# One kernel, the same 1738 operations in another order: linear attention and a squared-ReLU FFN on one NeuronCore

## The chip, the cores and the metric

The kernel runs on one core of one Trainium2 chip. The metric is the device time of one execution in microseconds, as the median over runs. Everything that follows is read from one profiled execution of the kernel before the change.

## What is computed

```python
def phi(x):                                   # x: (8, 8, 576, 64), w_phi: (64, 128)
    proj = np.einsum('bhsd,df->bhsf', x, w_phi)
    proj = proj - np.max(np.abs(proj), axis=-1, keepdims=True)
    return np.concatenate([np.exp(proj), np.exp(-proj)], axis=-1)
q_p, k_p = phi(q), phi(k)
kv  = np.einsum('bhsf,bhsd->bhfd', k_p, v)
z   = np.sum(k_p, axis=2)
num = np.einsum('bhsf,bhfd->bhsd', q_p, kv)
den = np.einsum('bhsf,bhf->bhs', q_p, z)[..., None] + 1e-06
x   = (num / den).transpose(0, 2, 1, 3).reshape(4608, 512)
h   = np.maximum(x @ w_in, 0.0)               # w_in: (512, 2048)
out = (h * h) @ w_out                         # w_out: (2048, 512)
```

Eight batches of 576 tokens with eight heads go through the attention, and all 4608 tokens then go through the FFN. Inputs and output are float32 in HBM; the matmuls run in bfloat16.

## The kernel before, in words

**Staging.** Each batch has 512 tokens in the main part and 64 at its end. The FFN works on nine chunks of 512 tokens: chunk c (0 to 7) is the main part of batch c, and chunk 8 gathers the 64-token ends of all batches (tile `xS`). While the attention of batch c + 1 runs, the FFN of chunk c runs between its pieces. TensorE takes both in one instruction stream.

**Attention of one batch.** k, q and v are loaded by GpSimd's queue (`load`, `load_q`; lines 245, 253, 265, 274) into double-buffered tiles `xk`, `xq`, `xv`, with a cast to bfloat16. k and q have to stand head dimension first. For batches 0 and 1 TensorE does that (L316, operations Txk and Txq, with copies Cxk and Cxq from PSUM by VectorE or ScalarE, L190 and L192). From batch 2 on one DMA transpose each on SyncE's queue does it (L326, Xxk and Xxq). `project` (L342; L369 and L494 in the first batch) multiplies with `w_phi`. Its contraction is only 64 deep, so its matmuls use 64 of the 128 rows, and two of them with different rows follow one another in pairs. The program calls such operations `tiled`: Pk, Pq, and Fq (L572). VectorE takes the maximum of absolute values (L376, L397, L501, L534: Mk, Mq), and ScalarE the two exponentials (L385, L403, L547, L587). ScalarE's em makes the factors of v, VectorE scales v with them (L430: V, V4), and KV (L458, L463) sums k features times v. NA and NB (L651; L602 in the first chunk) multiply the features of q with it; between them VectorE scales by en (L663: SA). VectorE then divides (L673, L677: rd, xo). The result is transposed into `xT`, by TensorE for batch 0 (L630, L693) and by a DMA transpose on SyncE's queue for the others (L711: Xx). For batches 4 to 7 the features of q are made token first and are transposed by a DMA as well (L551: Xf).

**FFN of one chunk.** F1 (L797) makes four accumulating matmuls of 128 x 512 into one PSUM bank. Relu (L774 on ScalarE or L776 on VectorE) moves the bank to `hr`, and VectorE squares it (L783). F2 (L891) makes four of the sixteen accumulating matmuls of an output tile; after the last, a copy to `ot` (three buffers, L190 or L192) and a store (L909, L906) follow on SyncE's queue. Chunk 0 goes in smaller pieces, f1a, f1b, f1 and f1p (L822, L808, L836), so that it can begin before the attention of batch 0 is done. The very last output tile is split in columns (L855, L869, L871, L878).

**What sets the order.** Nothing is scheduled while the kernel is built. Each piece of work is added to a `Plan` as an operation with a number (its `seq`), an engine, and the values that it reads and writes. Five tables at the end of the file then say what becomes of it:

- `ORDER` lists all 1738 operations. Each engine takes its own in that order, held by dependencies that `pin` adds (L135). Within one engine nothing overtakes.
- `BASES` gives each PSUM tile its bank (eight banks, shared by all uses).
- `STATES` says for each copy or relu that may run on either ScalarE or VectorE which of the two takes it.
- `GATES` makes a load of batches 2 to 7 wait for one named operation before GpSimd issues it.
- `FILL` puts matmuls on a zero tile (L964) ahead of some TensorE operations.

```python
def arrange(self):
    for op in self.ops:
        if op.alt is not None and STATES[op.group] == "1":
            op.eng, op.occ, op.lat = op.alt
    for g, b in zip(self.banks, BASES):
        g.base = int(b)
    return [self.ops[i] for i in ORDER]
```

The numbers used in the prediction: 85, 74, 50, 41 and 63 are the five k transposes of batch 0 on TensorE; 9 and 13 the loads of k that 41 and 63 read; 15 and 20 the two halves of q of batch 0; 329 is the first f1a. 315, 1079 and 1276 are Xx transposes, each the last or next to last of its chunk. 1178 is a load of v for batch 6, and 1295 a relu. 555 and 716 are output stores, 733 an output copy, and 1709 to 1723 the last stores ahead of the split tile's.

Of the kernel before, what the change touches and what calls it, by code (L numbers as in the profile page):

```python
# [107 lines left out]
def kernel(  # L108
# [952 lines left out]
)  # L1061
STATES = (
    '0000000101000111101000110010000000000000010000011100110000100010001000101001010001000010110010100010'
    '0000100100100101010000000000100100100001100100101000011101000000000100101011101000000100010110001000'
    '1101100110001011100000011011000'
)
GATES = {
# [46 lines left out]
```

## Time and profile before

| | |
|---|---|
| median of 3 runs | 354.33 us (352.88 to 354.97) |
| profiled execution, its own time | 353.94 us |
| its span, first to last instruction | 352.2 us |
| TensorE, VectorE, ScalarE, GpSimd busy | 97%, 76%, 66%, 27% of the span |
| moved by DMA | 49.05 MB, 139 GB/s over the span |
| mean granted TensorE clock | 0.995 |

The page gives busy time by engine and slice, the chain of work that ended last, and groups of instructions by source line. Views of the trace give windows, waits and the timeline. In the timeline a row has the start and the duration in us, then engine, line, operation and tiles, with the number of instructions that were merged into it; a matmul's duration includes its tail, so a row reaches beyond the start of the next. "SPq" and the like are issuing instructions. A line like L797 is that of kernel.py.

### The profile page before, as it was taken

How to read it: one execution, taken by the hardware profiler on the slowest of the kernel's cores; microseconds unless marked ns; L12 is line 12 of the kernel's file. 1: busy time of each engine (PE TensorE's matmuls, PEld its weight loads, DVE VectorE, ACT ScalarE, POOL GpSimd, SP SyncE). 2: the span in 40 equal slices, each digit the busy share in tenths (PEclk: the TensorE clock that was granted, in tenths of full speed). 3: DMA queues.
4: the chain of work that ended last, by engine and by line, in shares of the span. 5: the costliest groups of instructions: out<-in, count | busy, mean ns of one | idle time of the engine just before them, and what ended most of it. 6: DMA issues, size and time to landing. Idle time of an engine off the chain costs nothing.

```text
span 352.2 us, 8392 instructions
## 1 busy us (share of the span) xinstructions
PE 341.5 (97%) x3343; PEld 192.0 (55%) x3343; DVE 268.9 (76%) x513; ACT 233.3 (66%) x439; POOL 96.2 (27%) x144
## 2 busy tenths in 40 slices
PE   6999999999999999999999999999999999999995
PEld 6778866544644555445545555455555554444443
DVE  4899997889887989689979887877989653564150
ACT  3999997789885776976597785895596503212111
POOL 8673461282461636021421302040100000000000
PEclk9999999999999999999999999999999999999999
DMA  8999999999999899997999999999857431100115
GB/s 92 172 196 202 201 155 168 159 122 167 162 130 189 138 150 151 165 201 152 163 140 202 165 212 140 214 106 179 155 117 157 96 87 67 60 2 0 71 50 120
DMA packets 133623, 49.05 MB, mean 139 GB/s; under 512 B 102096, under 2 KB 129104, under 8 KB 133584
## 3 DMA queue, kind: packets, MB, share of 16 engines
q0 software_dynamic: 45232, 18.36, 46.0%
q1 hardware_dynamic: 88112, 29.99, 44.3%
q8 instruction: 26, 0.43, 0.5%
q10 hardware_dynamic: 240, 0.16, 0.2%
q14 instruction: 13, 0.11, 0.1%
HBM read 36.77 MB, written 9.44 MB: 131 GB/s over the span
## 4 chain that ended last, share of the span: by engine, by line
PE 77%; DVE 10%; ACT 5%; DMA 5%; issue 2%; SPq 0%; DVEq 0%; ACTq 0%; POOLq 0%
PE psum L797 27%; PE psum L891 27%; PE psum L651 4%; PE psum L458 4%; PE psum L342 4%; PE psum L836 2%; DMA out_dram<-ot 2%; DVE va L430 2%; DMA xT<-xo 2%; DVE mk L397 1%; ACT hr L774 1%; DMA xk<-in_k_dram 1%; DVE hr L776 1%; PE psum L572 1%; DVE h L783 1%
## 5 line engine op out<-in xcount | busy, mean ns | idle before, releaser
L891 PE MATMUL psum<-wout,h 128*128 128x512 bf16 x560 | 134.9, 379 | 0.2 <-ACT ot L192 0.2
L797 PE MATMUL psum<-xT,win 128*128 128x512 bf16 x448 | 106.9, 379 | 1.4 <-DVE hr L776 0.8
L774 ACT ACTIVATE hr<-psum 128x512 bf16<-128x512 f32 x103 | 59.8, 596 | 54.5 <-PE psum L797 36.8
L891 PEld LDWEIGHTS <-h 128*128 128x128 bf16 x560 | 50.4, 97 | 54.6 <-issue 0.9
L797 PEld LDWEIGHTS <-win 128*128 128x128 bf16 x512 | 47.6, 97 | 54.3 <-issue 2.7
L783 DVE TENSOR_TENSOR h<-hr 128x512 bf16<-128x512 bf16 x144 | 56.6, 415 | 20.6 <-ACT hr L774 19.8
L547 ACT ACTIVATE qf<-psum 128x1024 bf16<-128x1024 f32 (+1 forms) x40 | 36.5, 938 | 12.3 <-DVE mq L534 11.3
L397 DVE TENSOR_REDUCE mk<-psum 128x8 f32<-128x1024 f32 (+1 forms) x35 | 38.6, 1110 | 4.6 <-PE psum L342 4.5
L587 ACT ACTIVATE qpn<-psum 128x1024 bf16<-128x1024 f32 (+1 forms) x40 | 36.7, 938 | 5.7 <-PE psum L572 4.9
L403 ACT ACTIVATE kp<-psum 128x1024 bf16<-128x1024 f32 (+1 forms) x35 | 32.7, 935 | 9.3 <-DVE mk L397 9.2
L651 PEld LDWEIGHTS <-qpn 128*128 128x128 bf16 x624 | 27.8, 98 | 13.9 <-issue 1.0
L663 DVE TENSOR_TENSOR psum<-psum,en 128x520 f32<-128x520 f32 (+1 forms) x39 | 27.2, 701 | 9.5 <-PE psum L651 5.6
L776 DVE TENSOR_SCALAR hr<-psum 128x512 bf16<-128x512 f32 x41 | 27.8, 685 | 6.7 <-PE psum L797 6.2
L403 ACT ACTIVATE kn<-psum 128x1024 bf16<-128x1024 f32 (+1 forms) x35 | 32.8, 937 | 0.0
L651 PE MATMUL psum<-kv,qpn 128*128 128x65 bf16 x624 | 31.1, 193 | 0.0
L430 DVE TENSOR_TENSOR va<-xv,va 64x256 bf16<-64x256 bf16 (+2 forms) x66 | 30.1, 471 | 0.9 <-ACT va L422 0.2
L245 POOL DMA_DIRECT2D xv<-in_v_dram x27 | 19.7, 734 | 36.0 <-DVE h L783 11.8
L245 POOL DMA_DIRECT2D xk<-in_k_dram x28 | 20.6, 740 | 31.6 <-ACT va L422 20.0
L677 DVE TENSOR_TENSOR xo<-psum,rden 128x512 bf16<-128x512 f32 (+1 forms) x39 | 26.7, 686 | 1.4 <-DMA xT<-xo 0.7
L265 POOL DMA_DIRECT2D xq<-in_q_dram x24 | 17.4, 725 | 33.0 <-ACT hr L774 13.7
L534 DVE TENSOR_REDUCE mq<-psum 128x8 f32<-128x1024 f32 (+1 forms) x20 | 22.3, 1113 | 2.9 <-PE psum L342 2.7
L501 DVE TENSOR_REDUCE mq<-psum 128x8 f32<-128x1024 f32 (+1 forms) x20 | 22.0, 1111 | 0.9 <-PE psum L342 0.8
(79 smaller groups left out, 383.5 us busy)
## 6 DMA issues: line engine op xcount, KB each, us to landing
out_dram<-ot SPq DMA_DIRECT2D x32, 256.0 KB, 3.1
xk<-in_k_dram POOLq DMA_DIRECT2D x26, 128.0 KB, 4.6
xq<-in_q_dram POOLq DMA_DIRECT2D x24, 128.0 KB, 4.8
xv<-in_v_dram POOLq DMA_DIRECT2D x24, 128.0 KB, 4.5
win<-in_moe_w_in_dram POOLq DMA_DIRECT2D x4, 512.0 KB, 9.2
wout<-in_moe_w_out_dram POOLq DMA_DIRECT2D x4, 512.0 KB, 14.0
xq<-in_q_dram POOLq DMA_DIRECT2D x4, 256.0 KB, 7.1
out_dram<-ot SPq DMA_DIRECT2D x6, 128.0 KB, 2.4
```

Source lines behind the costliest of these rows:

```text
L245: pin(nc.gpsimd.dma_start(out=x[:, a * 512 : z * 512].rearrange("p (h x) -> p h x", x=4 * D), in_=src[b][2 * a : 2 * z, 0:512, :].rearrang ...
L397: pin(nc.vector.tensor_reduce(out=mk_view(g), in_=ps2(pj)[:, :, : n * Fd].rearrange("p e (i f) -> p e i f", f=Fd), axis=AX.X, op=ALU.max, ...
L403: pin(nc.scalar.activation(out=dst[slot][:, :, :n, :].rearrange("p e i f -> p e (i f)"), in_=ps2(pj)[:, :, : n * Fd], func=ACT.Exp, scale= ...
L430: pin(nc.vector.tensor_tensor(out=t[:, :, :D].rearrange("p m (x c) -> p m x c", c=2), in0=x.rearrange("p (m x c) -> p m x c", m=n, c=2), i ...
L547: pin(nc.scalar.activation(out=o, in_=i_, func=ACT.Exp, scale=sgn))
L587: pin(nc.scalar.activation(out=o, in_=i_, func=ACT.Exp, scale=sgn))
L651: pin(nc.tensor.matmul(out=o[:, u // 4, u % 4 * D1 : (u % 4 + 1) * D1], lhsT=qpn[slot][:, sg * half + u * m : sg * half + u * m + P], rhs= ...
L774: pin(nc.scalar.activation(out=hr[sl], in_=ps1(g), func=ACT.Relu))
L776: pin(nc.vector.tensor_scalar(out=hr[sl], in0=ps1(g), scalar1=0.0, scalar2=None, op0=ALU.max))
L783: pin(nc.vector.tensor_tensor(out=dst, in0=i_, in1=i_, op=ALU.mult))
L797: pin(nc.tensor.matmul(out=o, lhsT=win[mc // 4][:, kc, mc % 4 * P : (mc % 4 + 1) * P], rhs=x, start=(kc == 0), stop=(kc == KC - 1)))
L891: pin(nc.tensor.matmul(out=ps1(g), lhsT=h2[c % 2][mc // 4][:, mc % 4, tt * P : (tt + 1) * P], rhs=wout[mc // 4][:, mc % 4, :], start=(mc = ...
```

## The change

Only the five tables differ; no operation is added, removed or made larger. In `ORDER` nearly all of the 1738 entries stand elsewhere. The multiset of TensorE operations ahead of the first FFN operation (329) is the same in both. The filler matmuls go from 123 to 133. In `STATES`, relu goes from 103 on ScalarE and 41 on VectorE to 97 and 47, the kv copy from 22 and 10 to 24 and 8, and the copies of the transposed q of batches 0 and 1 from 6 and 4 to 5 and 5. All 108 entries of `GATES` differ. The beginnings of the tables show the kind of edit:

```diff
 ORDER = [
-    0, 1, 14, 11, 10, 9, 13, 4, 5, 2, 7, 3, 6, 12, 20, 85, 74, 15, 86, 50, 75, 87, 51, 18, 76, 88, 89, 52, 41, 54,
+    0, 1, 14, 11, 10, 15, 4, 3, 8, 2, 12, 9, 13, 85, 74, 20, 86, 50, 75, 6, 87, 51, 19, 52, 89, 88, 76, 54, 18, 5,
...
 GATES = {
-    377: 148, 378: 98, 379: 214, 380: 47, 381: 167, 382: 117, 383: 72, 384: 198, 385: 341, 386: 167, 387: 114,
+    377: 345, 378: 71, 379: 125, 380: 256, 381: 351, 382: 171, 383: 242, 384: 85, 385: 351, 386: 254, 387: 369,
...
 FILL = {
-    85: (0, 26), 87: (0, 4), 63: (7, 27), 65: (7, 10), 112: (7, 4), 108: (7, 3), 110: (7, 3), 116: (7, 23),
-    147: (0, 5), 144: (3, 5), 228: (5, 2), 139: (7, 7), 135: (7, 4),
+    85: (0, 26), 87: (1, 2), 41: (3, 8), 63: (7, 16), 106: (7, 9), 65: (7, 10), 116: (7, 37), 110: (7, 7),
+    144: (7, 3), 234: (7, 12), 122: (2, 3),
 }
```

`FILL` reads: ahead of operation 85, 26 filler matmuls into bank 0, and so on.

More of the change, by code (lines that the diff above doesn't have):

```diff
@@ L1056 @@
 BASES = (
-    '6416400204322513661766422322303066244004212225500116560364052321520063666262060671046174450554510220'
-    '0074766200632320030044545745044406625177535353421636126466346124271707562172030220124656661401142406'
-    '0521060023272401407337722555000322023644665716064116141117701024024564166263266207446420070114711526'
-    '2200223265026500450054435750413426075473330556731234357527705727215016742316316745263'
+    '3365011410546263026006250466754000264044240003231531412063222567402066002660360464771665542444330406'
+    '4040500244646266226435233153255376712411446266732264242066466004000176004171504413524624034176240540'
+    '4407333722404137367210660222064402460023664755476105576102654542033503163016224665520055501120415475'
+    '4662421310664640442500316413227100650641336171350747727221571503436702437242153704532'
 )
 STATES = (
-    '0000000101000111101000110010000000000000010000011100110000100010001000101001010001000010110010100010'
-    '0000100100100101010000000000100100100001100100101000011101000000000100101011101000000100010110001000'
-    '1101100110001011100000011011000'
+    '0001000111000110001000101000000000000010000000100000101100000011010000010110000010000000001001011000'
+    '0011111000100000000100111110000100000000010010000010100011100110000010010010000111100001000000011111'
+    '0010010100010111101011101101011'
 )
 GATES = {
[11 rows of a table removed]
[11 rows of a table added]
 }
 FILL = {
-    85: (0, 26), 87: (0, 4), 63: (7, 27), 65: (7, 10), 112: (7, 4), 108: (7, 3), 110: (7, 3), 116: (7, 23),
-    147: (0, 5), 144: (3, 5), 228: (5, 2), 139: (7, 7), 135: (7, 4),
+    85: (0, 26), 87: (1, 2), 41: (3, 8), 63: (7, 16), 106: (7, 9), 65: (7, 10), 116: (7, 37), 110: (7, 7),
+    144: (7, 3), 234: (7, 12), 122: (2, 3),
 }
```

184 rows, old and new, of tables (GATES, ORDER) are left out of this document.

## The prediction

> **What bounds the kernel now.** I read the page first: engine shares, slices and the chain of waits.
>
> ```profile
> span 352.2 us, 8392 instructions
> PE 341.5 (97%) x3343; PEld 192.0 (55%) x3343; DVE 268.9 (76%) x513; ACT 233.3 (66%) x439; POOL 96.2 (27%) x144
> ...
> PE   6999999999999999999999999999999999999995
> ...
> PE 77%; DVE 10%; ACT 5%; DMA 5%; issue 2%; SPq 0%; DVEq 0%; ACTq 0%; POOLq 0%
> ```
>
> TensorE is busy in all slices but the first and the last. Busy is not the same as working, since a matmul's tail counts too, so next come the windows by stage and TensorE's own waits.
>
> ```profile
> 0.00:5.70 5.70, 2.87 (x26) 2.69 (x26) 1.25 (x6) 1.28 (x1) 4.61 (x11) 1.00 0.64 73
> 5.70:16.00 10.30, 9.99 (x144) 8.70 (x144) 8.68 (x21) 8.31 (x22) 8.17 (x13) 0.83 1.43 157
> 16.00:28.60 12.60, 11.80 (x197) 8.69 (x198) 12.50 (x26) 12.56 (x26) 7.98 (x11) 1.00 1.43 197
> 28.60:245.00 216.40, 213.23 (x2266) 120.60 (x2262) 187.58 (x344) 172.29 (x319) 74.05 (x109) 1.00 1.14 165
> 245.00:352.20 107.20, 103.64 (x718) 51.35 (x716) 58.88 (x119) 38.80 (x74) 1.42 (x2) 1.00 0.36 83
> ```
>
> ```profile
> PE psum L316 <- DMA xk<-in_k_dram: 1.9, 1, 1.9
> PE psum L964 <- DVE warm L226: 1.0, 1, 1.0
> PE psum L797 <- DVE hr L776: 0.8, 2, 0.6
> PE psum L342 <- DVE xo L677: 0.5, 1, 0.5
> ```
>
> The columns of the windows are PE, PEld, DVE, ACT and POOL busy, then granted clock, DMA share and GB/s. There are two regimes. Up to 28.6 us VectorE (12.50 of 12.60) and ScalarE (12.56 of 12.60) are full, and TensorE fills its waits with 123 warming matmuls. Behind 28.6 us TensorE is idle for 3.2 of 216.4 us, and its listed waits are all below 1 us: there its instruction stream is the bound. 28.6 us is a landmark in both orders. At 28.64 the first FFN op (f1a, operation 329, L822) starts, and counted in the two orders, exactly the same TensorE operations stand ahead of it before and after the change.
>
> **The change, part by part.** The operations are the same 1738, so the terms are order, engines, fillers and gates.
>
> *Row-tiled blocks.* The timeline of TensorE shows what it costs to go from 128-row matmuls to 64-row ones (the projections, L342) and back:
>
> ```profile
> 250.98 1.02 PE L891 MATMUL psum<-wout,h 128*128 128x512 bf16 x4
> 251.84 0.41 PE L651 MATMUL psum<-kv,qpn 128*128 128x65 bf16 x8
> 252.09 1.02 PE L891 MATMUL psum<-wout,h 128*128 128x512 bf16 x4
> 253.05 0.40 PE L342 MATMUL psum<-wphi,qT 64*128 64x128 bf16 x8
> 253.28 0.39 PE L342 MATMUL psum<-wphi,kT 64*128 64x128 bf16 x8
> 253.50 0.39 PE L342 MATMUL psum<-wphi,qT 64*128 64x128 bf16 x8
> 253.82 5.36 PE L891 MATMUL psum<-wout,h 128*128 128x512 bf16 x24
> ...
> 28.64 0.61 PE L822 MATMUL psum<-xT,win 128*128 128x128 bf16 x8
> ...
> 344.98 3.66 PE L855 MATMUL psum<-wout,h 128*128 128x384 bf16 x32
> ```
>
> Four F2 matmuls take 251.84 - 250.98 = 0.86 us when 128-row work follows, and 253.05 - 252.09 = 0.96 when 64-row work follows. Eight projection matmuls take 0.22 to 0.23 within a block and 253.82 - 253.50 = 0.32 at its end. So each edge costs 0.10 us. The order before has 60 such blocks (120 edges), the order after 52 (104). Behind f1a, where TensorE is the bound, it is 104 edges before and 86 after, ahead of f1a 16 and 18. The gain is 18 x 0.10 = 1.8 us, on the path. The Trainium skill, "TensorEngine Tiling", Key Properties, says that a change of tiling mode drains the engine, and "TensorE: Matmul & The Clock Gate", Single matmul latency, gives a warm constant of about 166 ns beside the streaming. If that whole constant were paid at each edge, an estimate from that page would be 18 x 0.166 = 3.0 us and the forecast 1.2 us lower; the rows say 0.10.
>
> *TensorE's stretch behind f1a.* From 28.64 to the end of the last matmul, 344.98 + 3.66 = 348.64, are 320.0 us. Read as above (0.863 for each of the 268 ops of four 512-wide matmuls, 231.3 us; 73.1 us for the rest), the work is 304.4, the edges 10.4, so 5.2 us are waits, in some twenty pieces below 0.8 us. For the order after I counted how much TensorE work lies between an operation and the one that feeds it back over VectorE or ScalarE, and subtracted the bare durations of that chain. Distances with less than 0.6 us to spare are 81 before and 64 after, with less than 0.2 us 18 and 18. Waits in the trace are spread over all classes of spare, so I weigh each class with its waits before and get 0.2 us less. Taken: 304.4 + 8.6 + 5.0 = 318.0, that is 2.0 us less. As bounds I take 3 us (fewer middling distances) and 10 us (twice what this order has).
>
> *The start.*
>
> ```profile
> 8.07 2.82 PE L964 MATMUL psum<-warm 128*128 128x128 bf16 x27
> 10.73 0.39 PE L316 MATMUL psum<-ident,xk 128*128 128x128 bf16 x4
> ...
> 11.16 0.42 DVE L190 COPY kT<-psum 128x512 bf16<-128x512 bf16 x1 [1.01 <-PE psum L316]
> ...
> 20.66 0.63 ACT L192 ACTIVATE kT<-psum 128x512 bf16<-128x512 bf16 x1
> ```
>
> The first half of q (256 KB) now goes ahead of two pieces of k on POOL's queue. At the 157 GB/s of the second window that is 1.7 us for these pieces; the transpose at 10.73 had stood behind 27 fillers, not behind its data, so most of it is hidden, and the bound is 0 to 1 us. Two copies (kT, qT) move from VectorE (0.42 each) to ScalarE (0.63 each), one of them into ScalarE's time before its first Exp. Up to the copy that releases f1a, VectorE gets rid of 2 x 0.42 and takes on one more kT copy and one SA (L663), which stood behind it before; ScalarE has 1.3 us more, of which about a half lies in idle time. VectorE's wait of 1.01 us is there to be used. Together between -0.8 and +0.8 us: 0. The warming matmuls go from 123 to 133, all ahead of the first KV, where TensorE waits for the two others: 0, and 10 x 0.06 = 0.6 us without that cover.
>
> *Engines.* Six more relus (103 to 97 on ScalarE) go to VectorE, which has 28.8 us idle in the long window: 0 on the path, at most 6 x 0.69 us by the row of L776 below.
>
> ```profile
> L776 DVE TENSOR_SCALAR hr<-psum 128x512 bf16<-128x512 f32 x41 | 27.8, 685 | 6.7 <-PE psum L797 6.2
> ...
> L677 DVE TENSOR_TENSOR xo<-psum,rden 128x512 bf16<-128x512 f32 (+1 forms) x39 | 26.7, 686 | 1.4 <-DMA xT<-xo 0.7
> ...
> xv<-in_v_dram POOLq DMA_DIRECT2D x24, 128.0 KB, 4.5
> ...
> out_dram<-ot SPq DMA_DIRECT2D x32, 256.0 KB, 3.1
> ...
> L245 POOL DMA_DIRECT2D xv<-in_v_dram x27 | 19.7, 734 | 36.0 <-DVE h L783 11.8
> ...
> 158.45 0.69 DVE va L430
> ```
>
> *Gates and loads.* All loads of batches 2 to 7 get another place on POOL's queue and another gate. Taking for each load the latest gate ahead of it on the queue, the least TensorE work between that gate and the first user is 10.1 us after (the v piece 1178, gated on relu 1295) and 13.8 before. It needs the landing (4.5 us), an issue of 0.7 and a scaling of V of 0.7: 5.9. Spare 4.2 us, so 0. Stores move too: 555 (chunk 0) now stands behind 716 (chunk 1) on SP's queue, with 5 us of TensorE work from 716's place to the copy 733 that needs the same buffer; 716's own issue, 0.6 us, and the landing of 3.1 us fit, barely. Taken 0; if it is late, ScalarE waits up to 1 us and the relus behind 733 with it.
>
> *The end.*
>
> ```profile
> 346.87 1.12 SPq L906 DMA_DIRECT2D out_dram<-ot  x2
> ...
> 348.30 1.17 SPq L878 DMA_DIRECT2D out_dram<-otl  x2
> ```
>
> Each store takes 0.56 us of SP. After the change six of them (1709, 1708, 1722, 1723, 1716, 1715) queue up behind output copies of the last 4 us, and the last two stores (L878) go out up to 0.35 us later; ScalarE issues the other two and is 0.15 us later than SP now. Taken: +0.2, bounds 0 and 0.35.
>
> **Sum.** -2.0 + 0 + 0 + 0 + 0.2 = -1.8. The profiled execution took 353.94 us, so 352.1; the median of the runs shown lies 0.4 higher, so 352.5 us. A measurement of this kernel can tell about 0.5% (1.8 us) from no change.
>
> **The rivals.**
>
> *Fewer waits than counted.* If the waits fall to 3 us and the start uses VectorE's idle 1.01 us, it is 352.5 - 2.0 - 0.8 = 349.7. For it speaks the lower count of short distances; against it that they are one fifth lower, not two. Chance 0.16.
>
> *The saved edges come back as waits.* VectorE is busy for 187.6 of 216.4 us; where TensorE waits for it anyway, an edge costs nothing. Then 352.5 + 1.8 = 354.3. Against it: the listed waits of TensorE sum to a few us. Chance 0.12.
>
> *Another stretch at half clock.* The 27 fillers took 10.73 - 8.07 = 2.66 us, 0.10 each against 0.06 later, and the clock column says 0.83 in that window: 0.17 x 2 x 10.3 = 3.5 us at half, after TensorE had waited for the first k. With k later it can idle again before 10.5 us and get a second such stretch; it costs TensorE 1.7 us, of which the full VectorE and ScalarE hide some: +1.0, 353.5. The Trainium skill, "TensorE: Matmul & The Clock Gate", What's actually happening, has the clock halve after an idle window of about 3.4 us; the trace agrees with the length. Chance 0.08.
>
> *Transposes land too late (slower).* Each FFN chunk starts when the last transpose xT<-xo (L711, SP's queue) has landed. Rows of the timeline, of the chain and of the listing of L711:
>
> ```profile
> 212.51 0.41 PE L651 MATMUL psum<-kv,qpn 128*128 128x65 bf16 x8
> ...
> 214.27 1.19 SPq L711 DMA_TRANSPOSE xT<-xo  x1
> ...
> 221.32 3.61 PE psum L797 x16
> ...
> DMA to landing us min/median/max: 2.3/4.0/6.8
> ```
>
> From the end of those eight matmuls (0.25 us after 212.51) to the issue are 1.5 us, and with 4.0 to landing 5.5. TensorE work between that NB and the chunk's first F1 is, before and after: 7.8 and 7.1 us (transpose 315), 8.1 and 6.1 (1079, the one shown), 8.4 and 6.3 (1276); elsewhere it is above 7.3 or no shorter than before. At the median all three still fit. At the longest landing, 1.5 + 6.8 = 8.3, the three wait 1.2 + 2.2 + 2.0 = 5.4 us: 357.9. From a landing of 6.2 us on (waits of 3.6 in sum) the kernel is slower by over 0.5%. For it: the loads beside these transposes go at other times, and DMA is busy at 1.14 in the long window. Against it: a median of 4.0. Chance 0.22, times of 356.1 to 357.9.
>
> **How the numbers follow.** The forecast has 0.42, with a range of its own of 350.8 to 354.2 (waits of 3.3 to 6.7 us); about three quarters of that are below 352.56, which is 0.5% under 354.33. Faster by over 0.5%: 0.31 + 0.16 = 0.47. Within 0.5%: 0.11 + 0.12 + 0.08 = 0.31. Slower: 0.22. The range 349.2 to 357.4 leaves out a third of the first rival and a half of the last, less than 2 in 10.
>
> **What would show it.** Right: in TensorE's timeline 104 edges of 0.10 us, f1a at 28.6 plus or minus 0.8, 317 to 319 us from there to the last matmul's end, no new row over 1 us in TensorE's waits. Wrong: f1a behind 29.5; "PE psum L797 <- DMA xT" rows in the waits; a clock below 1.00 behind 10.5 us; VectorE or ScalarE rows of several us as TensorE's releasers; the last store over 1 us later behind the last matmul.

## The result and the profile after

The kernel after takes 351.08 us (median of 6 runs, 350.57 to 352.22), the kernel before 354.53 (6 runs beside them, 352.88 to 355.02). The ratio is 0.992, with a 95% interval of 0.9896 to 0.9943. A second set on another occasion gave 350.77 us and 0.9905 (0.9875 to 0.9936). The profiled execution of after took 351.15 us, its span is 349.2.

The page of after, engines and the chain:

```profile
span 349.2 us, 8405 instructions
PE 336.7 (96%) x3323; PEld 192.3 (55%) x3353; DVE 272.0 (78%) x518; ACT 229.6 (66%) x434; POOL 96.2 (28%) x144
...
PE 84%; DVE 7%; DMA 3%; ACT 3%; issue 2%; POOL 1%; POOLq 0%; DVEq 0%; ACTq 0%
```

TensorE's share of the chain rises from 77 to 84%, VectorE's falls from 10 to 7 and ScalarE's from 5 to 3: fewer steps of the chain go over an engine that TensorE has to wait for. (30 matmul records are missing here, 3323 beside 3353 weight loads, so TensorE's busy time is not compared.)

The windows (columns as before) and TensorE's longest waits behind the start:

```profile
5.70:16.00 10.30, 9.78 (x148) 8.57 (x149) 8.36 (x19) 8.47 (x23) 9.10 (x14) 1.00 1.51 161
16.00:28.60 12.60, 11.62 (x200) 9.23 (x200) 12.58 (x28) 12.30 (x27) 6.32 (x9) 1.00 1.36 201
28.60:245.00 216.40, 213.26 (x2283) 122.30 (x2304) 192.75 (x354) 173.09 (x324) 76.21 (x112) 1.00 1.11 167
```

```profile
PE psum L316 <- DMA xk<-in_k_dram: 2.3, 2, 2.0
PE psum L891 <- issue: 1.1, 7, 0.2
...
PE psum L572 <- ACT qpn L587: 0.5, 1, 0.5
...
PE psum L797 <- DMA xT<-xo: 0.2, 1, 0.2
```

The rows of before for a relu (L776, 0.8) and for xo (L677, 0.5) are gone; of waits for VectorE or ScalarE behind the start, the longest now is 0.5. (The row of L891 comes from the missing records: it is absent in the second set's trace, which has all of them.) Up to 28.6 us VectorE and ScalarE are as full as before (12.58 and 12.30 of 12.60). In the long window VectorE does 5.2 us more than before (192.75 against 187.58): 3.1 of it is more work over the whole span (272.0 against 268.9), the rest is work that moved in from the stretches before and behind.

The timeline of after at the landmarks of the prediction:

```profile
29.11 0.61 PE L822 MATMUL psum<-xT,win 128*128 128x128 bf16 x8
...
256.52 1.02 PE L797 MATMUL psum<-xT,win 128*128 128x512 bf16 x4
257.48 0.40 PE L342 MATMUL psum<-wphi,qT 64*128 64x128 bf16 x8
...
340.96 3.66 PE L855 MATMUL psum<-wout,h 128*128 128x384 bf16 x32
```

Four F1 matmuls ahead of a 64-row block take 257.48 - 256.52 = 0.96 us: the edge of 0.10 us as before. f1a starts 0.47 us later, the last matmul ends at 340.96 + 3.66 = 344.62 instead of 348.64.

To split the 3.0 us between the spans I laid TensorE's matmuls of each trace beside the order and took the differences of starts: what exceeds the bare step of the work (216 ns for a 512-wide matmul, and so on) is an edge where the rows change, and a wait elsewhere.

| us | f1a starts | edges behind it | waits behind it | last operation of TensorE starts | from there to the end | span |
|---|---|---|---|---|---|---|
| before | 28.64 | 10.40 | 5.42 | 348.25 | 3.9 | 352.2 |
| after | 29.11 | 8.60 | 2.74 | 344.24 | 5.0 | 349.2 |
| after, second set | 29.17 | 8.60 | 1.91 | 343.47 | 5.0 | 348.5 |
| difference of the first two | +0.46 | -1.80 | -2.68 | -4.0 | +1.0 | -3.0 |

The useful work behind f1a is 303.8 us in every row. So 1.8 us come from the edges and 2.7 from waits; 0.5 is given back at the start and 1.0 at the end. The fall of the waits is not one execution's: worked out in the same way, before with a single relu moved (below) has 5.5, and the executions of after with small edits of its start or end have 1.5 to 2.7.

### The profile page after: what moved, and what is told of

Its sections match the earlier page's. It is cut to its first block, busy times and chain, and to the rows that moved or that the text cites. A ratio compares the mean times of both kernels' runs of the same rounds, so it can differ in the third digit from the quotient of the medians.

```text
span 349.2 us, 8405 instructions
## 1 busy us (share of the span) xinstructions
PE 336.7 (96%) x3323; PEld 192.3 (55%) x3353; DVE 272.0 (78%) x518; ACT 229.6 (66%) x434; POOL 96.2 (28%) x144
## 4 chain that ended last, share of the span: by engine, by line
PE 84%; DVE 7%; DMA 3%; ACT 3%; issue 2%; POOL 1%; POOLq 0%; DVEq 0%; ACTq 0%
PE psum L891 32%; PE psum L797 31%; PE psum L651 5%; PE psum L342 5%; PE psum L458 4%; DVE va L430 2%; PE psum L836 2%; DMA xk<-in_k_dram 1%; DMA xT<-xo 1%; PE psum L572 1%; PE psum L822 1%; PE psum L808 1%; DVE mq L501 1%; PE psum L855 1%; PE psum L463 1%
## 5 line engine op out<-in xcount | busy, mean ns | idle before, releaser
L891 PE MATMUL psum<-wout,h 128*128 128x512 bf16 x530 | 129.6, 379 | 2.3 <-issue 1.1
L774 ACT ACTIVATE hr<-psum 128x512 bf16<-128x512 f32 x97 | 56.5, 598 | 53.9 <-PE psum L797 28.4
L891 PEld LDWEIGHTS <-h 128*128 128x128 bf16 x560 | 50.7, 97 | 54.9 <-issue 0.6
L776 DVE TENSOR_SCALAR hr<-psum 128x512 bf16<-128x512 f32 x47 | 32.0, 686 | 19.2 <-PE psum L797 17.7
L651 PE MATMUL psum<-kv,qpn 128*128 128x65 bf16 x624 | 30.2, 193 | 0.2
L677 DVE TENSOR_TENSOR xo<-psum,rden 128x512 bf16<-128x512 f32 (+1 forms) x39 | 26.7, 686 | 1.0 <-DVE rden L673 0.2
L192 ACT ACTIVATE ot<-psum 128x512 f32<-128x512 f32 x20 | 12.0, 598 | 17.8 <-PE psum L891 15.8
```

The costliest lines, as they stand in the source:

```text
L651: pin(nc.tensor.matmul(out=o[:, u // 4, u % 4 * D1 : (u % 4 + 1) * D1], lhsT=qpn[slot][:, sg * half + u * m : sg * half + u * m + P], rhs= ...
L774: pin(nc.scalar.activation(out=hr[sl], in_=ps1(g), func=ACT.Relu))
L776: pin(nc.vector.tensor_scalar(out=hr[sl], in0=ps1(g), scalar1=0.0, scalar2=None, op0=ALU.max))
L891: pin(nc.tensor.matmul(out=ps1(g), lhsT=h2[c % 2][mc // 4][:, mc % 4, tt * P : (tt + 1) * P], rhs=wout[mc // 4][:, mc % 4, :], start=(mc = ...
```

## The experiments

**What an edge costs.** Two kernels add one matmul on the zero tile ahead of each of 32 F1 operations of chunk 8, with 128 rows or with 64:

```diff
+        if op.seq in EDGES:
+            now[0] = filler
+            pin(nc.tensor.matmul(out=psum[:, op.opens[0].base, :P], lhsT=warm[:ROWS], rhs=warm[:ROWS], start=True, stop=True))
         now[0] = op
         op.fn()
```

> The kernel after, with one more matmul of 128 rows on the zero tile ahead of each of the 32 F1 operations of the last chunk (its result is overwritten by the F1 that follows). No tiling edge is added. Both theories: 32 x 0.056 = 1.8 us more than the kernel after, 352.9 us. It is the control for the kernel with 64 rows.

> The same 32 additional matmuls, at the same places, with 64 rows instead of 128: between 128-row neighbours each brings two edges, 64 in all. My theory (0.10 us an edge, as the timeline of before had it): 6.4 us more than the control with 128 rows, about 359.3 us. Rival 1 (an edge pays the whole constant of a matmul, 0.166): 10.6 us more than the control, 363.5. Rival 2 (edges cost nothing in a dense stream, and the 0.10 read in the timeline is only how ends are modelled): within 0.5 us of the control.

Measured: 353.68 us with 128 rows (ratio to before 0.9977, 0.9954 to 1.0), 360.8 with 64 (1.018, 1.0138 to 1.0222). The difference of 7.1 us over 64 edges is 0.11 each; from the two intervals it is uncertain by about 1.7 us, 0.03 per edge. The timelines, first with 128 rows, then with 64:

```profile
318.94 0.22 PE L967 MATMUL psum<-warm 128*128 128x128 bf16 x1
318.99 1.03 PE L797 MATMUL psum<-xS,win 128*128 128x512 bf16 x4
319.86 1.03 PE L891 MATMUL psum<-wout,h 128*128 128x512 bf16 x4
320.72 0.22 PE L967 MATMUL psum<-warm 128*128 128x128 bf16 x1
```

```profile
319.94 0.23 PE L967 MATMUL psum<-warm 64*128 64x128 bf16 x1
320.10 1.04 PE L797 MATMUL psum<-xS,win 128*128 128x512 bf16 x4
320.97 1.03 PE L891 MATMUL psum<-wout,h 128*128 128x512 bf16 x4
321.93 0.23 PE L967 MATMUL psum<-warm 64*128 64x128 bf16 x1
```

Into the 64-row matmul: 321.93 - 320.97 = 0.96 against 320.72 - 319.86 = 0.86. Out of it: 0.16 against 0.05. Both edges cost 0.10 us, in the time of the kernel and not only in the records. The 0.166 of rival 1 and the zero of rival 2 are excluded (10.6 and 0 us, against 7.1 with 1.7).

**One wait alone.** Before's largest single wait behind f1a, 0.76 us, ended when a relu (operation 521, L776) was done. By TensorE's starts its bank was full at 83.58 us, but three other operations stood ahead of it on VectorE:

```profile
83.61 1.01 DVE L430 TENSOR_TENSOR va<-xv,va 64x256 bf16<-64x256 bf16 x2
84.55 0.42 DVE L783 TENSOR_TENSOR h<-hr 128x512 bf16<-128x512 bf16 x1
84.88 0.68 DVE L776 TENSOR_SCALAR hr<-psum 128x512 bf16<-128x512 f32 x1
...
85.62 1.02 PE L797 MATMUL psum<-xT,win 128*128 128x512 bf16 x4 [0.60 <-DVE hr L776]
```

```diff
-            if op.alt is not None and STATES[op.group] == "1":
+            if op.alt is not None and (STATES[op.group] == "1") != (op.seq == 521):
```

> The kernel before, with one relu (operation 521, chunk 0) on ScalarE instead of VectorE; nothing else. In before it was ready at 83.6 us and stood on VectorE behind scalings of V and a square until 84.88; TensorE waited for it until 85.62 (0.76 us start to start, the largest single wait of that kernel). ScalarE was idle for 0.53 us at that time. My theory (the waits that went are queues of VectorE and ScalarE at single operations, set by the order and the engine): the wait falls below 0.2 us and the rest of TensorE's stream moves up, the span is 0.5 to 0.8 us shorter, 352.9 us or so. Rival (the stream is full of waits that take over): another wait of 0.5 us or more appears within the next ten microseconds, and the span is the same within 0.2 us.

Measured: 353.53 us beside 354.0 of before, ratio 0.9998 (0.998 to 1.0017). The wait at that F1 fell from 0.76 to 0.10 us, and TensorE's next operation took it over with 0.71, as these rows of ScalarE's and TensorE's timelines show:

```profile
83.60 1.09 ACT L774 ACTIVATE hr<-psum 128x512 bf16<-128x512 f32 x2
84.56 0.26 ACT L422 ACTIVATE va<-mk 128x32 bf16<-128x32 f32 x1
84.85 0.60 ACT L774 ACTIVATE hr<-psum 128x512 bf16<-128x512 f32 x1
85.35 1.02 ACT L403 ACTIVATE kn<-psum 128x1024 bf16<-128x1024 f32 x1
...
86.42 0.40 PE L342 MATMUL psum<-wphi,qT 64*128 64x128 bf16 x8 [0.65 <-ACT kn L403]
```

The relu is the second of the two at 83.60. From there ScalarE's queue has no gap up to the end of the exponential kn (85.35 + 1.02 = 86.37), and the projection needs the bank that kn reads. My theory was right on the wait and wrong on the time; the rival holds on the wait that takes over. (The span, 352.6 us, is 0.4 longer than before's, not equal within 0.2; f1a starts 0.35 later in this execution.) Here a single move shifted the wait to the other engine's queue.

**All engine choices.** The order, banks, gates and fillers of after with the `STATES` of before (111 of 231 entries differ):

```diff
+STATES = (
+    '0000000101000111101000110010000000000000010000011100110000100010001000101001010001000010110010100010'
...
```

> The kernel after, with the engines (ScalarE or VectorE) of before for every relu and copy; order, banks, gates and fillers stay those of after. My theory (waits of TensorE come from the fit of order and engine, operation by operation): 1 to 3 us slower than after, with new waits for relus or copies on ScalarE and VectorE. Rival (the order alone carries the gain, the engine choice is slack): within 0.5 us of after.

Measured: 365.71 us, ratio 1.0346 (1.0293 to 1.04), 14.6 us slower than after where 1 to 3 were expected. In its profiled execution f1a starts at 31.78 us, and the waits behind it, worked out as above, are 17.8 us. (This execution is the longest of the four, 368.89 us.) TensorE's list of waits, and a window right behind the start:

```profile
PE psum L797 <- DVE hr L776: 2.2, 4, 1.1
...
PE psum L797 <- ACT hr L774: 1.5, 3, 1.0
...
PE psum L651 <- DVE kv L190: 0.8, 1, 0.8
PE psum L572 <- DVE mq L501: 0.7, 2, 0.4
```

```profile
30.40:37.30 6.90, 6.78 (x63) 5.53 (x60) 4.71 (x11) 4.07 (x6) 2.81 (x4) 0.51 1.40 200
```

They are relus, copies and maxima of both engines, some fifty waits, none above 1.2 us. About 2.7 of the 17.8 us, an estimate from the starts of the matmuls, are not waits: in the window shown the granted clock is 0.51, and the first f1a takes 1.00 us where after has 0.54. Why the clock fell there was not shown; TensorE was busy for 13.65 of the 14.4 us before it. That leaves 15 us of waits. The order has no low waits of its own; order and engines fit each other or they don't. The rival (engine choice is slack) is out by far.

**The gates.** `GATES` emptied, in after and in before:

```diff
+GATES = {}
```

> The order after without any gate on a load. Theory (loads have several us of room, and the 2.7 us fewer waits behind the first FFN operation come from the order of the three compute engines): waits stay within 1 us, 350.5 to 352 us. Rival (the waits are fewer because the gates fit the landings): most of the 2.7 us come back, 353 to 354 us, with rows of TensorE or VectorE that wait for a transpose or a load.

> The order before without any gate on a load. Theory (gates matter little in either order): 353.5 to 355.5 us. Rival (the order before waits because its gates let loads go at the wrong time): faster by 1 to 3 us, 351.5 to 353.5 us.

Measured: 369.67 us for after without gates (1.0471, 1.0444 to 1.0497), 18.6 us slower than with them; 376.41 for before without (1.068, 1.0616 to 1.0744), whose runs, from 372.99 to 379.51, are 19.6 to 26.1 us slower than before beside them (353.37). Both theories are far off, and so are both rivals. TensorE's waits in after without gates, a window of it, and the landings of the feature transposes (L551) without gates and with them:

```profile
PE psum L342 <- ACT qf L547: 4.8, 2, 4.6
PE psum L797 <- DMA xT<-xo: 3.8, 2, 2.1
PE psum L797 <- ACT qf L547: 2.6, 1, 2.6
PE psum L651 <- ACT kv L192: 2.3, 1, 2.3
```

```profile
163.00:170.00 7.00, 4.68 (x40) 2.92 (x40) 4.14 (x9) 5.10 (x12) 0.00 (x0) 0.51 0.68 126
```

```profile
DMA to landing us min/median/max: 3.0/4.8/14.3
```

```profile
DMA to landing us min/median/max: 3.1/5.2/7.0
```

The median landing hardly changes; the longest goes from 7.0 to 14.3 us (in before from 8.4 to 13.7). ScalarE's exponentials qf then wait for these transposes, 16.0 us in five waits in after without gates, and in after not at all. The lost time stands in a few places: in after without gates 7.8 us between 160 and 180 and 8.4 between 200 and 220.

Not all of it is waiting. The granted clock is 0.51 between 163 and 170 us, behind the wait of 4.6, and 0.79 between 200 and 216; at half clock the four matmuls of an F1 take 1.70 us (167.22 to 168.92) instead of 0.86. By the starts, an estimate, some 5 of the 18.6 us are matmuls at half clock. A wait of several us cost more than its own length here.

I read the rest as loads that go out early and hold up transposes on the same DMA engines. Just ahead of the longest wait GpSimd issues nine loads from 146.55 us on, where after with gates issues one at 149.00 and seven from 151.01 on, which fits; which load meets which transpose was not shown. That the two sets of gates are worth different amounts isn't shown either.

**The warming matmuls.** Only the first group is kept (26 of 133):

```diff
+FILL = {85: FILL[85]}
```

> The order after with only the first 26 of its 133 filler matmuls. Theory (the fillers lie in waits of TensorE and keep its clock up): without them a second stretch at half clock, the first FFN operation 0.5 to 1.5 us later, 351.6 to 352.6 us. Rival (fillers stand in the way, since the first FFN operation came 0.46 us later with ten more of them): 0.3 to 0.6 us faster, about 350.6 us.

Measured: 350.81 us (0.9921, 0.9899 to 0.9943), the same as after. In the profiled execution f1a starts at 29.95, 0.84 later than in after, and the waits behind it are 1.52 instead of 2.74, so the span is 348.9. Two rows from it:

```profile
16.35 1.01 PE L316 MATMUL psum<-ident,xq 128*128 128x128 bf16 x8
17.29 1.03 PE L494 MATMUL psum<-wphi,qT 64*128 64x128 bf16 x8
```

These eight transposes take 17.29 - 16.35 = 0.94 us, with an edge of 0.1 in it; in after they take 17.19 - 16.74 = 0.45. The half clock that the theory feared did come: this trace's first clock record, to full speed, is at 23.77 us, that of after at 9.14. But it cost nothing that the times show. The 0.84 us at f1a can't be put down to it either, since executions with after's own stream ahead of f1a have it anywhere from 28.64 to 30.95.

**The end.** In after the two stores 1716 and 1715 stand behind 1709 on SyncE's queue, and 1709 waits for ScalarE's copy. Moved ahead of it:

```diff
+for s in (1716, 1715):
+    ORDER.remove(s)
+    ORDER.insert(ORDER.index(1709), s)
```

> The order after, with the two stores 1716 and 1715 ahead of 1709 on SP's queue, since their copy is done 0.8 us earlier. Theory (the end is held by the queue of six stores on SP, ready ones behind one that waits): SP is free 0.9 us earlier, the last two stores go out as soon as their copies are done, and 0.7 to 1.0 us of the 1.04 us lost behind the last matmul come back: about 350.2 us. Rival (the end is set by the landing of the stores that ScalarE issues, or by the last matmul alone): no change, 351.1 us.

> The kernel after, unchanged, beside the three others on the same chip. All theories: 351.1 us, ratio to before 0.992, within its interval of 0.9896 to 0.9943.

> The kernel after with the stores 1716 and 1715 ahead of 1709 on SyncE's queue, a second time, now beside the kernel after on the same chip. My theory (the store of the last tile stands behind a store whose copy is late): 0.8 to 1.0 us shorter than after, all of it behind TensorE's last operation. Rival (the 1.6 us of the first time was TensorE's waits for landings, which vary from execution to execution): within 0.5 us of after.

Measured: 349.49 us (0.9885, 0.9864 to 0.9906) the first time, 350.16 (0.9899, 0.9853 to 0.9944) beside 350.77 of after the second time. The timelines of the end, of after and of the edited kernel:

```profile
340.35 0.60 ACT L192 ACTIVATE ot<-psum 128x512 f32<-128x512 f32 x1 [4.63 <-PE psum L891]
...
340.97 3.73 SPq L906 DMA_DIRECT2D out_dram<-ot  x6
...
344.29 1.34 ACTq L878 DMA_DIRECT2D out_dram<-otl  x2
...
345.12 1.10 SPq L878 DMA_DIRECT2D out_dram<-otl  x2
```

```profile
338.46 3.72 SPq L906 DMA_DIRECT2D out_dram<-ot  x6
...
342.59 1.40 ACTq L878 DMA_DIRECT2D out_dram<-otl  x2
342.61 1.14 SPq L878 DMA_DIRECT2D out_dram<-otl  x2
```

In after all six stores leave once the copy at 340.35 is done (340.95), and SyncE's last store starts at 345.12, 0.83 us behind ScalarE's, which carries the other half of the same tile. In the edited kernel the two start together. From the start of TensorE's last operation to the end it is 4.1 and 4.3 us in its two executions, and 4.1 in the one with both edits of the next experiment, against 5.0 and 5.0 in after: 0.7 to 0.9 us are there each time. In the medians the saving was 1.6 us (against after of another set) and 0.6 (beside it); the second difference is within the intervals, so the time alone does not settle it.

**The start.** The first half of q back behind two pieces of k, alone and with the edit of the end:

```diff
+ORDER.remove(15)
+ORDER.insert(ORDER.index(13) + 1, 15)
```

> The kernel after with the first half of q (operation 15) behind the two pieces of k (9 and 13) on GpSimd's queue, as in before. My theory (k's pieces, issued 1.2 us later than in before, delay the first transposes): the first FFN operation starts at 28.6 instead of 29.1 us, and the kernel is 0.3 to 0.5 us shorter than after. Rival (ScalarE and VectorE are full by then, and q is wanted at once): the first FFN operation starts at 29.1 or later, the kernel is the same or up to 1.2 us longer.

> Both edits together on the kernel after: the stores 1716 and 1715 ahead of 1709, and the first half of q behind the two pieces of k. If the two terms are independent (one at the start, one at the end), the saving is the sum of the two: by my theories 1.1 to 1.5 us shorter than after, about 349.8 us. By the rivals, within 0.5 us of after or longer.

Measured: 351.3 us (0.9923, 0.9892 to 0.9953) alone, 350.36 (0.9894, 0.9861 to 0.9926) with both, beside 350.77 of after. f1a starts at 28.88 and 28.87. That would be 0.3 us earlier than in after, but the kernel with the edit of the end alone, which has the same start as after, had it at 28.64 in one execution and at 29.49 in another. The question is open: single executions differ by more than the edit could bring, and the medians show nothing. Both edits together are 0.4 us below after, where the theories had 1.1 to 1.5. Of the versions tried, that with the edit of the end has the lowest medians, without being separated from after in the second set.

## Why the prediction was right and where it was wrong

The time (352.5 forecast, 351.08 measured) lies in the range, on the faster side. Part of that is luck: against the sum, the waits brought 2.5 us more than forecast, while the end cost 0.8 and the start 0.5 more, and these misses partly cancel. One sign of being right was missed: from f1a to the last matmul's end it was to be 317 to 319 us, and it is 344.62 - 29.11 = 315.5.

*Edges: right.* 18 fewer behind f1a at 0.10 us, 1.8 us. The addition of 64 edges elsewhere gave 0.11 with an uncertainty of 0.03. That saved edges come back as waits did not happen: the waits fell as well.

*Waits: the term that was mis-sized.* The forecast had 5.2 to 5.0; measured were 5.4 and 2.7, with 1.9 in a second execution. The failed step is the weighing: I counted how much TensorE work lies between an operation and its feedback, subtracted bare durations, and gave each class of spare the waits that it had before. That leaves out what stands ahead in VectorE's or ScalarE's queue. The relu at 84.88 shows it: its own chain is 0.68 us, its queue 1.3. Waits of this kind recur at the same operations with the same size, even without gates, where these operations come 3.6 to 19 us later:

| us, at operation | 564 | 711 | 795 | 914 | 1298 |
|---|---|---|---|---|---|
| before | 0.76 | 0.34 | 0.33 | 0.32 | 0.52 |
| before, no gates | 0.76 | 0.34 | 0.33 | 0.32 | 0.52 |
| after | 0.12 | below 0.06 | below 0.06 | below 0.06 | below 0.06 |

These five are 2.27 us before and at most 0.4 after. They do not depend on the gates. All five operations open a PSUM bank, and by the trace each waits for the last reader of that bank's use before: 521 (a relu), 740 (a relu), 806 (an exponential), 927 (a relu) and 1091 (xo). Not each stood in a queue: ScalarE idled for 0.34 us ahead of 740, until a square on VectorE was done. By the tables of after, the first still follows 521, which ScalarE now takes; the other four open a bank that another operation has emptied (629, 679, 966 and 1196). So the banks have a part in it: 330 of the 385 entries of `BASES` differ, and no run changed them alone. What share of the 2.7 us each table has stays open.

After has recurring ones of its own (0.35, 0.26, 0.25 and 0.20), 1.06 in all. Another 1.06 us (0.42 and 0.64, at 73.8 and 75.6 us) stands in one execution of after, the first of them behind a transpose xT<-xo, and not in the second. So on the waits what happened is the rival "fewer waits than counted": its 3 us of waits are near the 2.7, and its gain at the start did not come.

*Start: in its bounds.* 0 within 0.8 was forecast, +0.46 measured; executions of one stream differ by as much anyway.

*End: mis-sized.* +0.2 with a bound of 0.35 was forecast, +1.0 measured. The queue of six stores was named, but priced with 0.56 us each as if its head could leave early; the row says 3.73 / 6 = 0.62 each, all behind one copy, and 0.42 from there to the start of the next store.

*Transposes too late: did not happen.* The forecast's slower side asked for landings above 6.2 us at three places; one wait for a transpose is listed, 0.2 us, at another place.

*Gates at zero: nothing speaks against it, but the reason is only half of it.* No load was late. But I priced gates by the loads' own spare; without any gates each kernel loses 18.6 us or more, though no load is then held back.

*Fillers and engines at zero.* For the fillers this holds within 0.3 us of the median. For the engines the reason ("VectorE, which has 28.8 us idle") was wrong: the same order with other engines costs 14.6 us. Idle time of an engine says little on where a queue stands.

## What to carry to other kernels

In a stream in which one engine is 97% busy, look for its small waits at single operations in two executions: those that recur at the same operation point at the bank that it opens and at what holds up the engine that empties it. Here moving one operation only moved the wait; order, engines and banks, changed together, took most of it away. In a dense stream, count the changes between 64-row and 128-row matmuls and multiply by the 0.10 us found here, and price a queue of stores from the copy that its head waits for. Where a wait grows to several us, look at the granted clock behind it too.

## What was not expected of the hardware

*How long TensorE runs at half clock at the start differs between executions of one stream.* In the profiled execution with 32 fillers of 128 rows, whose stream ahead of f1a is that of after, f1a started at 30.95 us, and this was the longest of its ten runs (355.68 us, median 353.68). A window and its timeline:

```profile
5.70:16.00 10.30, 9.52 (x121) 8.25 (x122) 6.75 (x16) 6.64 (x18) 8.80 (x13) 0.67 1.54 160
```

```profile
9.51 1.91 PE L964 MATMUL psum<-warm 128*128 128x128 bf16 x16
11.22 0.63 PE L316 MATMUL psum<-ident,xk 128*128 128x128 bf16 x4
```

Sixteen fillers take 11.22 - 9.51 = 1.7 us here, 0.107 each. In after the same sixteen go at 0.056:

```profile
9.94 1.06 PE L964 MATMUL psum<-warm 128*128 128x128 bf16 x16
10.84 0.39 PE L316 MATMUL psum<-ident,xk 128*128 128x128 bf16 x4
```

A clock of 0.67 in that window is 0.33 x 2 x 10.3 = 6.8 us at half, twice the 3.5 us of before's 0.83. So half clock behind 10.5 us, as in the prediction's rival of another stretch, does occur; it came here in an execution and not with a change of the stream. It fits "TensorE: Matmul & The Clock Gate", What's actually happening, in the Trainium skill: the activity window of about 3.4 us runs freely and doesn't start with the kernel, so the point of change depends on where in it the first matmul falls. By an estimate from that page two windows would be 6.8 us; the trace agrees.

*The clock column can't be read ahead of a trace's first clock record.* There it shows 1.00 also while matmuls go at half rate. The first ten transposes of k, in the two executions of after:

```profile
5.90 1.25 PE L316 MATMUL psum<-ident,xk 128*128 128x128 bf16 x10 [1.96 <-DMA xk<-in_k_dram]
```

```profile
6.00 0.85 PE L316 MATMUL psum<-ident,xk 128*128 128x128 bf16 x10 [2.04 <-DMA xk<-in_k_dram]
```

The first trace's record to full speed comes at 9.14 us, the second's at 4.68, and f1a starts at 29.11 and 29.17. With the half clock up to 23.77 us of the kernel with 26 fillers, f1a was at 29.95. So the half clock alone does not set f1a, and how much of the 30.95 us it accounts for was not shown.
